# q and k of tiles 4 to 15 by seven products a pair, softmax and h lows partly on POOL, in an attention and MLP kernel

## The chip, the cores and the metric

The kernel runs on one core of one Trainium2 chip. The core has a matrix engine (PE; its weight loads are listed as PEld), a vector engine (DVE), an activation engine (ACT), a general engine (POOL, GpSimd) and SyncE (SP), which here only issues DMAs; ACT issues some as well. Each engine works through its own list of instructions in order. The metric is the device time of one execution in microseconds (us); the three runs of the kernel before have a median of 498.23 us (497.23 to 498.86).

## The reference, cut to what matters

```python
def _A_ref(x, wqkv, wo):                       # x: [1, 2048, 512]
    H = 32; Dh = D // H; W, dil = 8, 2         # 32 heads of 16
    q, k, v = split(x @ wqkv)
    ... # position s sees s, s-2, ... s-14
    logits = einsum("bhsd,bhswd->bhsw", q, kg) * Dh ** -0.5
    attn = softmax(where(mask, logits, -1e9))
    return einsum("bhsw,bhswd->bhsd", attn, vg) @ wo

def _B_ref(x, w1, b1, w2, b2):                 # 1792 hidden
    h = x @ w1 + b1
    return relu(h) ** 2 @ w2 + b2

xn = _layernorm(x)
return x + _A_ref(xn, wqkv, wo) * silu(_B_ref(xn, w1, b1, w2, b2))
```

## The kernel before

The 2048 rows are cut into 16 tiles of 128. To keep fp32 accuracy, every operand of a product is split into a high part (rounded by ACT to the matrix engine's fp32r) and a low part, the rest (a subtraction, mostly on DVE). A product is then three matmuls (`PASSES`): high by high, high by low, low by high.

**The pair stage.** For each tile the statistics and the normalised x are made, x is transposed (from tile 4 on: four DMAs that move blocks, `shuffle`, then a 32x32 block transpose on DVE, `trans`), split into high and low (`lowx`), and multiplied by the weights of q, k and v: 12 matmuls of 128x512 each (`qkv`). Tiles are worked on in pairs; two tiles together are a unit of 256 rows, whose q, k and v go to DRAM (`sq`, `sk`, `sv`).

**Attention** runs on DVE alone, unit by unit. For one unit there are four slices for the logits (`qk`: a 128x2048 multiply `pr`, then a reduce into `L`), the softmax (`soft_a`: row maximum `mx`, subtraction, exp on ACT; `soft_b`: row sum `sm`, reciprocal, product), and four slices for the weighted sum (`av`: a multiply `pv`, a reduce into `v`). The finished unit is stored to DRAM (`so`), loaded again in another layout (`oq`, four DMAs, `load_o`), transposed on DVE (`trans_o`, tiles `pT`), split (`lowo`, tiles `oT`) and multiplied by wo on PE (`out_product`, tiles `pw`).

**The MLP stage.** Four chunks of 512 rows, each over 14 blocks f of the hidden layer: `up` (12 matmuls into `ph`; then relu, square into the high part of `h` and the full square on ACT), `lowh` (the low part of h, on DVE), `down` (12 matmuls into the four banks `pb`, two blocks behind). At the end of a chunk the four gates are made (z = pb + b2 on DVE, silu on ACT); later z is multiplied by `pw` on DVE and x is added on POOL, and the result stored. Blocks 0 and 1 of the first chunk run in the last pair.

**What sets the order.** Each engine keeps the order in which the code calls it. The attention is a generator (`attention`); `pump` takes steps from it as long as a running count of DVE's work is not ahead of PE's. So the place of an attention step in DVE's list is fixed when the program is built, by that count.

The weights w1 and w2 of a block are loaded into four shared buffers (`piece`) and split once; the blocks below NKEEP = 6 during the pairs, the others in the first chunk.

Of the kernel before, what the change touches and what calls it, by code (L numbers as in the profile page):

```python
# [14 lines left out]
P = 128  # L15
# [20 lines left out]
NKEEP = 6  # L36
# [14 lines left out]
def body(ctx: ExitStack, tc: tile.TileContext, x, wqkv, wo, w1, b1, w2, b2, out):  # L51
# [38 lines left out]

    const = ctx.enter_context(tc.tile_pool(name="const", bufs=1))
# [3 lines left out]
    keep = ctx.enter_context(tc.tile_pool(name="keep", bufs=1))  # L95
    hpool = ctx.enter_context(tc.tile_pool(name="ph", bufs=1))
# [24 lines left out]
    ident = const.tile([P, P], F32, name="ident")  # L121
# [4 lines left out]

    p1ctx = ExitStack()
    px, pstg, pwq, pxT = (p1ctx.enter_context(tc.tile_pool(name=n, bufs=1)) for n in ("px", "pstg", "pwq", "pxT"))
    xins = {}
# [6 lines left out]
    def load_x(t):  # L136
        xins[t] = px.tile([P, D], F32, name=f"x{t}", tag="x", bufs=4)
        dma(xins[t], tile_rows(x, t))

    wq = [pwq.tile([P, 2, KT, 512], FR, name=f"wq{s}") for s in range(3)]  # L140
# [15 lines left out]
    def wq_parts(s, kt):  # L156
        return wq[s][:, 0, kt], wq[s][:, 1, kt], raws[s, kt]
# [66 lines left out]
    def attention():  # L224
# [30 lines left out]
        def soft_a(u, h=None):  # L255
            yield 1500
            m = part(u, h)
            L, n = Ls[u][:, m], m.stop - m.start
            if u == 0:
                i = slice(m.start // 8, m.stop // 8)  # L260
                lm = L.rearrange("p (i h) w -> p i h w", h=8)
                V.tensor_add(lm, lm, mask[:, i, None, :].to_broadcast([P, n // 8, 8, W]))
            mx = att.tile([P, n], F32, name=f"mx{u}_{h}", tag="mx")
            V.tensor_reduce(out=mx, in_=L, axis=AX.X, op=OP.max)
            V.tensor_sub(L, L, mx[:, :, None].to_broadcast([P, n, W]))

            def exp():
                A.activation(L, L, AF.Exp)
                exps.add((u, h))

            defer(clock["V"] + BEHIND, exp)

        def soft_b(u, h=None):
            while (u, h) not in exps:
                yield None
            yield 2100
# [90 lines left out]
    def load_w(pool, f):  # L367
        w12[f] = pool.tile([P, 2, 2, 512], FR, name=f"w{f}")

        r1, r2 = (p2.tile([P, 512], F32, name=f"{n}{f}", tag="xr", bufs=2) if f in (6, 9) else piece(f"{n}{f}")  # L370
                  for n in ("w1r", "w2r"))
# [4 lines left out]
    def split_w(f, eng=G):  # L376
        for i, r in enumerate(raws.pop(f)):
            split(w12[f][:, 0, i], w12[f][:, 1, i], r, eng)
# [3 lines left out]
    mv, means, rs, shifts, xn, xb, pTs, xt, xT, seen = ({} for _ in range(10))  # L382

    def moments(t, st):
        mv[t] = px.tile([P, 2], F32, name=f"mv{t}", tag="mv", bufs=2)
        rs[t] = px.tile([P, 1], F32, name=f"rs{t}", tag="rs", bufs=3)
        V.bn_aggr(mv[t], st)
        V.tensor_scalar_add(rs[t], mv[t][:, 1:2], 1e-5)
        G.tensor_tensor(rs[t], rs[t], mhalf, op=OP.pow)

    def small(name, t):
        return px.tile([P, 1], F32, name=f"{name}{t}", tag=name, bufs=3)

    def scratch(t):
        return px.tile([P, D], F32, name=f"scratch{t}", tag="scratch")

    def mean(t):
        means[t] = small("mean", t)
        A.activation(scratch(t), xins[t], AF.Copy, accum_out=means[t])
        G.tensor_scalar(means[t], means[t], -1.0 / D, None, op0=OP.mult)  # L400

    def spread(t):
        rs[t], shifts[t] = small("rs", t), small("shift", t)
        A.activation(scratch(t), xins[t], AF.Square, bias=means[t], accum_out=rs[t])
# [9 lines left out]
    def norm(t):  # L414

        src = xins.pop(t)
        if t < TURN:
            xn[t] = dst = px.tile([P, 2, D], F32, name=f"xn{t}", tag="xn", bufs=2)[:, 0]
# [11 lines left out]
        if t + 4 < NT:  # L430
            load_x(t + 4)
# [7 lines left out]
    def shuffle(t):  # L439

        src = xn.pop(t)
        xb[t] = px.tile([P, 4, 2, P], F32, name=f"xb{t}", tag="xn", bufs=2)
        for a in range(4):
            dma(xb[t][32 * a:32 * a + 32].rearrange("p b e c -> p b (e c)"), src[:, a].rearrange("p e c -> p (e c)"))

    def trans(t):
# [6 lines left out]
        else:  # L453
# [3 lines left out]
            seen[t] = clock["V"] + 800  # L457
        A.activation(xt[t][:, 0], pTs[t].rearrange("p (k n) -> p k n", k=KT), AF.Copy)

    def lowx(t):  # L460
        not_before(seen.pop(t))
        V.tensor_sub(xt[t][:, 1], pTs.pop(t).rearrange("p (k n) -> p k n", k=KT), xt[t][:, 0].bitcast(F32))

    stgs = {}

    def qkv(t, s, between=None, late=False):
# [5 lines left out]
        for n, (kt, a, b) in enumerate(order):  # L472
            PE.matmul(ps, xt[t][:, a, kt], wq[s][:, b, kt, :], start=n == 0, stop=n == 11)
# [4 lines left out]
    def evacuate(t, s, ps):  # L478
        if t % 2 == 0:
            stgs[s] = pstg.tile([P, 4, 2, P], F32, name=f"stg{t}_{s}", tag="stg", bufs=4)  # L480
        A.activation(stgs[s][:, :, t % 2], ps.rearrange("p (g c) -> p g c", g=4), AF.Copy,
                     scale=0.25 if s == 0 else 1.0)
        if t % 2:
            r0 = (t - 1) * P + (0 if s == 0 else HALO)
            dst = (sq, sk, sv)[s][:, r0:r0 + UP, :].rearrange("g (p e) c -> p g (e c)", e=2)
            dma(dst, stgs[s].rearrange("p g e c -> p g (e c)"))
            done = done_tiles["qkv"[s]]
            done[0] = t + 1
            done[1][t // 2] = clock["PE"]
# [8 lines left out]
    def up(c, f):  # L498
# [12 lines left out]
        A.activation(ph, ph, AF.Square)  # L511
        hs[f] = h, ph, clock["PE"] + 2000

    def lowh(f):
        h, ph, t = hs[f]
        not_before(t)
        V.tensor_sub(h[:, 1], ph, h[:, 0].bitcast(F32))
# [21 lines left out]
    x0 = scratch(0)  # L539
# [25 lines left out]
    for f in range(2):  # L565
        load_w(keep, f)
# [4 lines left out]
    lowx(2)  # L571
    qkv(1, 0, lambda: highs(2, 2))
    trans(3)
    lows(2, 2)
    lowx(3)
    stats(4)
    stats(5)
    next(stream)
    qkv(0, 2)
    norm(4)  # L580
    norm(5)
    shuffle(4)
    split_w(0, V)
    pump(LATE)
    qkv(1, 2)
    split_w(1, V)
    pump(LATE)
    for a in range(2, NT, 2):
        b, more = a + 1, a + 2 < NT
        later = a + 4 < NT  # L590

        def weights(f):
            if 2 <= f < NKEEP:
                load_w(keep, f)
            if 2 <= f - 1 < NKEEP:
                split_w(f - 1)

        if later:
            mean(a + 4)
        qkv(a, 0)  # L600
        if a + 2 < TURN:
            trans(a + 2)
        if later:
            spread(a + 4)
            mean(b + 4)
        pump(LATE)
        qkv(b, 0)
        weights(a - 5)
        if a + 2 < TURN:
            lowx(a + 2)  # L610
            trans(b + 2)
        elif more:
            trans(a + 2)
        if later:
            norm(a + 4)
            spread(b + 4)
        pump(LATE)
        qkv(a, 1)
        if a + 2 < TURN:
            lowx(b + 2)  # L620
        elif more:
            lowx(a + 2)
            trans(b + 2)
        if later:
            norm(b + 4)
            shuffle(a + 4)
        pump(LATE)
        if not more:
            up(0, 0)
        qkv(b, 1)  # L630
        if TURN <= a + 2 < NT:
            lowx(b + 2)
        if not more:
            pump()
            up(0, 1)
            lowh(0)
        weights(b - 5)
        pump(LATE)
        qkv(a, 2)
        pump(LATE)  # L640
        qkv(b, 2)
        if a == NT - 4:
            dma(b1t, b1.rearrange("(f p) -> p f", p=P))
        if a >= TPC:
            for t in (a, b):
                dma(sx[t // TPC][:, t % TPC], xt.pop(t).bitcast(F32))
        pump(LATE if more else -SLACK)
# [73 lines left out]
    dma(b2t, b2[None, :].to_broadcast([P, D]))  # L721

    for c in range(NCH):
# [4 lines left out]
        for f in range(2, NF):  # L728
            if c == 0:
                for i in (6, 7) if f == 2 else (f + 5,):  # L730
                    if i < NF:
                        load_w(p2, i)
            up(c, f)
            pump()
            if c == 0 and f == 3:
# [6 lines left out]
            if c == 0:  # L742
                if NKEEP <= f + 3 < NF:
                    split_w(f + 3)
# [100 lines left out]
```

## Time and profile before

| | |
|---|---|
| median of three runs | 498.23 us (497.23 to 498.86) |
| the profiled execution | 495.58 us |
| its span, first to last instruction | 493.8 us |
| mean granted PE clock | 0.998 |
| pair stage, to the end of the last pair | about 146 us |
| first gate of chunk 0, 1, 2 on DVE | 220.8, 305.8, 392.8 us |
| last attention reduce ends | 460.5 us |

The profile gives for every engine its busy time, in windows if asked; the chain that ended last, which follows each wait back to what released it; groups of equal instructions with their mean; and the single instructions in order of time, each with its start, its duration and the idle time before it. In these rows a name such as `pr<-k,q` says which tile is written from which others, without buffer numbers.

### The profile page before, as it was taken

How to read it: one execution, taken by the hardware profiler on the slowest of the kernel's cores; microseconds unless marked ns; L12 is line 12 of the kernel's file. 1: busy time of each engine (PE TensorE's matmuls, PEld its weight loads, DVE VectorE, ACT ScalarE, POOL GpSimd, SP SyncE). 2: the span in 40 equal slices, each digit the busy share in tenths (PEclk: the TensorE clock that was granted, in tenths of full speed). 3: DMA queues.
4: the chain of work that ended last, by engine and by line, in shares of the span. 5: the costliest groups of instructions: out<-in, count | busy, mean ns of one | idle time of the engine just before them, and what ended most of it. 6: DMA issues, size and time to landing. Idle time of an engine off the chain costs nothing.

```text
span 493.8 us, 5860 instructions
## 1 busy us (share of the span) xinstructions
PE 487.5 (99%) x2154; PEld 401.1 (81%) x2154; DVE 431.7 (87%) x370; ACT 211.0 (43%) x377; POOL 97.9 (20%) x105
## 2 busy tenths in 40 slices
PE   8999999999999999999999999999999999999997
PEld 5888888888888888887888888888888888888886
DVE  5925798998999999998999998899999889999445
ACT  5636455563343665316333324432252354313331
POOL 1311015571000779300112000112100011220000
PEclk9999999999999999999999999999999999999999
DMA  7999979769977892653406408043241805030222
GB/s 287 297 287 341 304 238 313 225 238 323 372 228 262 203 274 65 202 212 118 127 31 216 181 22 329 4 164 123 85 161 43 328 2 202 1 127 1 85 85 86
DMA packets 48520, 88.79 MB, mean 180 GB/s; under 512 B 5372, under 2 KB 32364, under 8 KB 45676
## 3 DMA queue, kind: packets, MB, share of 16 engines
q1 hardware_dynamic: 44172, 54.87, 35.3%
q10 hardware_dynamic: 4320, 33.56, 19.1%
q8 instruction: 17, 0.28, 0.2%
q14 instruction: 11, 0.09, 0.1%
HBM read 57.94 MB, written 27.32 MB: 173 GB/s over the span
## 4 chain that ended last, share of the span: by engine, by line
PE 83%; DVE 9%; issue 4%; ACT 2%; DMA 1%; ACTq 0%; POOL 0%; DVEq 0%; POOLq 0%
PE pq L80 27%; PE ph L80 24%; PE pb L80 24%; PE pw L80 8%; DVE v L80 2%; DVE pr L80 2%; DVE h L80 2%; DVE pv L80 1%; DMA x<-in_A_x 1%; ACT ph L80 0%; DVE sm_None L80 0%; ACT z L80 0%; DVE z L80 0%; ACT h L80 0%; PE pxT L80 0%
## 5 line engine op out<-in xcount | busy, mean ns | idle before, releaser
L80 PE MATMUL pb<-w,h 128*128 128x512 f32 x672 | 160.6, 389 | 0.0
L80 PEld LDWEIGHTS pb<-w,h 128*128 128x128 f32 x672 | 126.1, 188 | 26.2
L80 PE MATMUL ph<-xU,w 128*128 128x512 f32 x504 | 120.7, 389 | 0.3 <-DVE h L80 0.3
L80 PEld LDWEIGHTS ph<-xU,w 128*128 128x128 f32 x504 | 94.6, 188 | 20.2 <-DVE h L80 0.7
L80 ACT ACTIVATE ph<-ph,b1t 128x512 f32<-128x512 f32 x56 | 37.0, 661 | 163.0 <-PE ph L80 158.4
L80 PE MATMUL pq<-wq,xt 128*128 128x512 f32 x432 | 98.7, 390 | 0.0
L80 PEld LDWEIGHTS pq<-wq,xt 128*128 128x128 f32 x432 | 81.0, 188 | 17.2 <-ACT stg L80 0.3
L80 DVE TENSOR_TENSOR pr<-k,q 128x2048 f32<-128x2048 f32 x32 | 75.4, 2356 | 0.3
L80 DVE TENSOR_TENSOR pv<-v,L 128x2048 f32<-128x2048 f32 x32 | 73.8, 2305 | 0.4
L80 DVE TENSOR_REDUCE L<-pr 128x128 f32<-128x2048 f32 x32 | 72.9, 2279 | 0.6
L80 DVE TENSOR_REDUCE v<-pv 128x256 f32<-128x2048 f32 x32 | 72.9, 2279 | 0.6
L80 POOL TENSOR_TENSOR z<-z,xr 128x512 f32<-128x512 f32 x12 | 23.2, 1936 | 214.7 <-DVE z L80 209.9
L80 DVE TENSOR_TENSOR h<-ph,h 128x512 fp32r<-128x512 f32 x56 | 38.3, 683 | 19.9 <-ACT ph L80 19.9
L80 PE MATMUL pw<-wot,oT 128*128 128x512 f32 (+1 forms) x204 | 45.9, 376 | 0.0
L80 PEld LDWEIGHTS pw<-wot,oT 128*128 128x128 f32 x204 | 36.8, 188 | 7.1
L80 PE MATMUL ph<-xT,w 128*128 128x512 f32 x168 | 40.7, 391 | 0.0
L80 ACT ACTIVATE stg<-pq 128x512 f32<-128x512 f32 x48 | 27.2, 595 | 26.4 <-PE pq L80 16.9
L80 PEld LDWEIGHTS ph<-xT,w 128*128 128x128 f32 x168 | 31.5, 188 | 7.0 <-DVE h L80 0.4
L80 ACT ACTIVATE h<-ph 128x512 fp32r<-128x512 f32 x56 | 33.7, 601 | 1.8
L80 ACT ACTIVATE ph<-ph 128x512 f32<-128x512 f32 x56 | 33.3, 595 | 0.0
L80 PE MATMUL pq<-wq,xT 128*128 128x512 f32 x132 | 31.7, 398 | 0.0
L80 POOL TENSOR_TENSOR w<-w1r,w 128x512 fp32r<-128x512 f32 x12 | 18.9, 1577 | 57.1 <-DMA rwo<-in_A_wo 48.8
(66 smaller groups left out, 309.9 us busy)
## 6 DMA issues: line engine op xcount, KB each, us to landing
k<-sk ACTq DMA_DIRECT2D x8, 1408.0 KB, 8.1
v<-sv ACTq DMA_DIRECT2D x8, 1408.0 KB, 8.3
sx<-xt SPq DMA_DIRECT2D x12, 512.0 KB, 5.5
xU<-sx ACTq DMA_DIRECT2D x6, 1024.0 KB, 5.4
x<-in_A_x SPq DMA_DIRECT2D x16, 256.0 KB, 5.0
sk<-stg SPq DMA_DIRECT2D x8, 512.0 KB, 7.1
sq<-stg SPq DMA_DIRECT2D x8, 512.0 KB, 5.6
q<-sq ACTq DMA_DIRECT2D x8, 512.0 KB, 8.4
```

Of the source, the lines that this page charges most:

```text
L80: return tc.keep_in_program_order(f(*a, **k))
```

## The change

Four parts.

1. For the pairs of tiles 4 to 15, q and k come from seven half-size products (`SEVEN`, `pair_of_seven`) in place of eight. The two tiles are the rows, the halves of the 512 inputs the inner blocks, q and k the columns of a 2x2 block product. Needed are four sums of x blocks (`sums`: 128x256 each on DVE, split again by `high_sums` and `low_sums`), four sums of weight blocks (made once, on DVE), and seven additions of 128x512 for each pair (five on DVE out of PSUM, two on POOL). v is computed as before.
2. The work for later tiles is put into six steps of a pair by a table (`plan`), and the sums of the next pair are made one pair ahead.
3. The statistics from tile 6 on take the mean's factor on ACT, and no POOL operation for it (`spread`).
4. Blocks of x are loaded sooner and in order on SP (`queue`, `load_x` in `shuffle`); statistics and norms of tiles 4 and 5 are made earlier; the buffers of the q, k and v weights are used again for w1 and w2 (`HOME`), which are loaded and split two blocks ahead (`next_w`).

In the MLP stage the low part of h is made on POOL for chunks 1 to 3, from a copy of the square in SBUF (`hf`), and for whole units the softmax's subtraction and product go to POOL. The factor 0.25 of the logits moves from q into the exp.

```diff
         def soft_a(u, h=None):
-            V.tensor_sub(L, L, mx[:, :, None].to_broadcast([P, n, W]))
+            (G if h is None else V).tensor_sub(L, L, mx[:, :, None].to_broadcast([P, n, W]))
...
         def soft_b(u, h=None):
-            V.tensor_mul(L, L, sm[:, :, None].to_broadcast([P, n, W]))
+            (G if h is None else V).tensor_mul(L, L, sm[:, :, None].to_broadcast([P, n, W]))
...
+    def next_w():
+        f = len(w12)
+        if f < NF:
+            w12[f] = buffer(f"w{f}", HOME[f]) if f in HOME else p2.tile([P, 2, 2, 512], FR, name=f"w{f}")
+            for i, r in enumerate(raws.pop(f)):
+                split(w12[f][:, 0, i], w12[f][:, 1, i], r, G)
+            if f + 2 < NF:
+                load_w(f + 2)
...
+    def sums(a, half):
+        f, (pa, pb) = Sf[a], quarters(a)
+        if half == 0:
+            not_before(seen[a, "copy"])
+            V.tensor_add(f[:, 0], f[:, 3], pb[:, 1])
+            V.tensor_sub(f[:, 1], f[:, 0], pa[:, 0])
+        else:
+            V.tensor_sub(f[:, 2], pa[:, 0], f[:, 3])
+            V.tensor_sub(f[:, 3], pa[:, 1], f[:, 1])
...
+    def product(a, n, lhs, w):
+        ps = psA(f"pm{a}_{n}")
+        k = 0
+        for i in range(2):
+            for p, q in PASSES:
+                PE.matmul(ps, lhs(p, i), wq[w][:, q, i, :], start=k == 0, stop=k == 5)
+                k += 1
...
     def up(c, f):
-        A.activation(ph, ph, AF.Square)
-        hs[f] = h, ph, clock["PE"] + 2000
...
+        full = hpool.tile([P, 512], F32, name=f"hf{c}_{f}", tag="hf") if c else ph
+        A.activation(full, ph, AF.Square)
+        if c:
+            G.tensor_sub(h[:, 1], full, h[:, 0].bitcast(F32))
+        hs[f] = h, None if c else ph, clock["PE"] + 2000
...
     norm(3)
     lowx(2)
+    stats(4)
     qkv(1, 0, lambda: highs(2, 2))
     trans(3)
+    stats(5)
+    norm(4)
     lows(2, 2)
+    norm(5)
+    shuffle(4)
     lowx(3)
...
+    def pair_of_seven(a):
...
+        q, k = stgs[0], stgs[1]
+        p = product(a, 1, part_x(a, 0), Q0)
+        A.activation(q[:, :, 0], p, AF.Copy)
+        p = product(a, 5, part_s(a, 0), T1)
+        A.activation(k[:, :, 1], p, AF.Copy)
+        beside(a, 0)
+        p = product(a, 6, part_s(a, 1), T2)
+        not_before(clock["PE"])
+        V.tensor_add(k[:, :, 0], q[:, :, 0], p)
+        p = product(a, 2, part_x(a, 1), Q1)
+        beside(a, 1)
+        not_before(clock["PE"])
+        V.tensor_add(q[:, :, 0], q[:, :, 0], p)
+        p = product(a, 7, part_s(a, 2), T3)
+        not_before(clock["PE"])
+        V.tensor_add(q[:, :, 1], k[:, :, 0], p)
+        G.tensor_add(k[:, :, 0], k[:, :, 0], k[:, :, 1])
+        G.tensor_add(k[:, :, 1], k[:, :, 1], q[:, :, 1])
+        p = product(a, 3, part_s(a, 3), K1)
+        beside(a, 2)
+        qkv(a, 2)
+        not_before(clock["PE"] - 12 * MATMUL)
+        V.tensor_add(k[:, :, 0], k[:, :, 0], p)
+        store_qkv(b, 1)
+        beside(a, 3)
+        p = product(a, 4, part_x(b, 1), T4)
+        beside(a, 4)
+        not_before(clock["PE"])
+        V.tensor_add(q[:, :, 1], q[:, :, 1], p)
+        store_qkv(b, 0)
+        if last:
+            for f in range(2):
+                up(0, f)
+                pump()
+            lowh(0)
+        qkv(b, 2)
+        beside(a, 5)
```

(`beside(a, step)` makes what the table has for that step and pumps.) Three places of the programs show how instructions move. First PE's list at the pair of tiles 4 and 5: `pq4_0` is q of tile 4, `pm4_5` the fifth product of the pair that begins with tile 4, `S4_0` the first two sums of x. Before:

```order
L80 MATMUL pq4_0_537<-wq0_111,xt4_440 128x512 x12
L80 MATMUL pq5_0_564<-wq0_111,xt5_471 128x512 x12
L80 MATMUL pq4_1_596<-wq1_112,xt4_440 128x512 x12
L80 MATMUL pq5_1_625<-wq1_112,xt5_471 128x512 x12
L80 MATMUL pq4_2_645<-wq2_113,xt4_440 128x512 x12
L80 MATMUL pq5_2_662<-wq2_113,xt5_471 128x512 x12
```

And of the change:

```order
L84 MATMUL pm4_1_586<-wq0_111,xt4_473 128x512 x6
L84 MATMUL pm4_5_594<-wq6_117,S4_0_530 128x512 x6
L84 MATMUL pm4_6_606<-wq7_118,S4_0_530 128x512 x6
L84 MATMUL pm4_2_614<-wq1_112,xt4_473 128x512 x6
L84 MATMUL pm4_7_643<-wq8_119,S4_1_561 128x512 x6
L84 MATMUL pm4_3_653<-wq3_114,S4_1_561 128x512 x6
L84 MATMUL pq4_2_676<-wq4_115,xt4_473 128x512 x6
L84 MATMUL pq4_2_676<-wq5_116,xt4_473 128x512 x6
L84 MATMUL pm4_4_699<-wq9_120,xt5_476 128x512 x6
L84 MATMUL pq5_2_727<-wq4_115,xt5_476 128x512 x6
L84 MATMUL pq5_2_727<-wq5_116,xt5_476 128x512 x6
```

Four times 12 matmuls for q and k became seven times 6, and the second product of the pair already needs the sums.

Second, DVE's list at the first gate, the end of chunk 0: `z0_0` is the gate of its first tile, `v2` and `pv2` belong to attention unit 2. Before:

```order
L80 TENSOR_TENSOR pv2_3_1982<-v2_1650,L2_1245 128x4x2x256
L80 TENSOR_REDUCE v2_1650<-pv2_3_1982 128x256
L80 TENSOR_REDUCE sm3_None_2012<-L3_1626 128x64
L80 RECIPROCAL sm3_None_2012<-sm3_None_2012 128x64
L80 TENSOR_TENSOR L3_1626<-L3_1626,sm3_None_2012 128x512
L80 TENSOR_TENSOR z0_0_2017<-pb0_0_1440,b2t_1438 128x512
```

And of the change:

```order
L84 TENSOR_REDUCE v1_1747<-pv1_1_2035 128x256
L84 TENSOR_TENSOR pv1_2_2062<-v1_1747,L1_1374 128x4x2x256
L84 TENSOR_TENSOR z0_0_2064<-pb0_0_1484,b2t_1483 128x512
L84 TENSOR_TENSOR z0_1_2067<-pb0_1_1485,b2t_1483 128x512
L84 TENSOR_TENSOR z0_2_2070<-pb0_2_1486,b2t_1483 128x512
L84 TENSOR_TENSOR z0_3_2073<-pb0_3_1487,b2t_1483 128x512
L84 TENSOR_REDUCE v1_1747<-pv1_2_2062 128x256
L84 TENSOR_TENSOR pv1_3_2115<-v1_1747,L1_1374 128x4x2x256
L84 TENSOR_REDUCE v1_1747<-pv1_3_2115 128x256
```

The attention stands one unit further back at this place: unit 1 is being finished where unit 2 was done.

Third, DVE's list where the output of unit 6 is transposed for tiles 12 and 13 (`pT12<-oq6`), in chunk 3. Before, the last reduce of unit 6 (`v6`) stands 15 rows ahead of the transposes, and these rows lead up to them:

```order
L80 TENSOR_TENSOR pv7_1_3588<-v7_3376,L7_3140 128x4x2x256
L80 TENSOR_REDUCE v7_3376<-pv7_1_3588 128x256
L80 TENSOR_TENSOR h3_8_3572<-ph3_8_3559,h3_8_3572 128x512
L80 TENSOR_TENSOR pv7_2_3621<-v7_3376,L7_3140 128x4x2x256
L80 TENSOR_REDUCE v7_3376<-pv7_2_3621 128x256
L80 TENSOR_TENSOR h3_9_3605<-ph3_9_3592,h3_9_3605 128x512
L80 STREAM_TRANSPOSE pT12_3642<-oq6_3538 128x4x4x32
L80 STREAM_TRANSPOSE pT13_3646<-oq6_3538 128x4x4x32
```

And of the change:

```order
L84 TENSOR_TENSOR pv6_3_3733<-v6_3496,L6_3108 128x4x2x256
L84 TENSOR_REDUCE v6_3496<-pv6_3_3733 128x256
L84 TENSOR_REDUCE sm7_None_3737<-L7_3432 128x64
L84 RECIPROCAL sm7_None_3737<-sm7_None_3737 128x64
L84 STREAM_TRANSPOSE pT12_3777<-oq6_3741 128x4x4x32
L84 STREAM_TRANSPOSE pT13_3781<-oq6_3741 128x4x4x32
```

The transposes now stand two rows behind the last reduce of the unit that they transpose, and the h lows between the slices are gone from DVE's list. The same place for units 2 to 5 has three or four rows between.

More of the change, by code (lines that the diff above doesn't have):

```diff
@@ L137, in load_x, with buffer @@
         xins[t] = px.tile([P, D], F32, name=f"x{t}", tag="x", bufs=4)
-        dma(xins[t], tile_rows(x, t))
-    wq = [pwq.tile([P, 2, KT, 512], FR, name=f"wq{s}") for s in range(3)]
+        queue(xins[t], tile_rows(x, t))
+    def buffer(name, i):
+        return wts.tile([P, 2, 2, 512], FR, name=name, tag=f"b{i}")
+    wq = [buffer(f"wq{i}", i) for i in range(10)]
     raws = {}
@@ L365, in body, with load_w @@
     w12 = {}
[L367 to L371, printed above, removed]
+    def load_w(f):
+        r1, r2 = (piece(f"{n}{f}") for n in ("w1r", "w2r"))
         dma(r1.rearrange("p (k c) -> p k c", c=P), w1[:, f * P:(f + 1) * P].rearrange("(k p) c -> p k c", p=P))
@@ L441, in shuffle, with trans @@
         src = xn.pop(t)
[L442 removed]
+        xb[t] = px.tile([P, 4, 2, P], F32, name=f"xb{t}", tag="xb", bufs=2)
         for a in range(4):
[L444 to L446 removed]
+            queue(xb[t][32 * a:32 * a + 32].rearrange("p b e c -> p b (e c)"), src[:, a].rearrange("p e c -> p (e c)"))
+        for i in range(6 if t == TURN else t + 4, min(t + 6, NT)):
+            load_x(i)
+    def trans(t, then=True):
         place(t)
@@ L564, in body @@
     constants()
-    for f in range(2):
-        load_w(keep, f)
     qkv(0, 0, lambda: highs(2, 0))
@@ L584, in body, with at @@
+    sum_weights = [(wq[w][:, 0, i], wq[w][:, 1, i], raws[s, kt + i])
+                   for w, (s, kt) in ((T1, (0, 0)), (T2, (1, 2)), (T3, (1, 0)), (T4, (0, 2))) for i in range(2)]
+    for w in sum_weights[:4]:
+        split(*w, V)
     pump(LATE)
     qkv(1, 2)
-    split_w(1, V)
+    for w in sum_weights[4:]:
+        split(*w, V)
     pump(LATE)
+    plan = {}
+    def at(a, step, f, *args):
+        if args[0] < NT:
+            plan.setdefault((a, step), []).append((f, args))
     for a in range(2, NT, 2):
[L589 to L605, printed above, removed]
-        pump(LATE)
[L607 to L635, printed above, removed]
-            lowh(0)
-        weights(b - 5)
-        pump(LATE)
-        qkv(a, 2)
-        pump(LATE)
-        qkv(b, 2)
@@ new lines, in body, with beside @@
+    for t in range(6, NT, 2):
+        for i, (a, step) in enumerate({6: ((2, 0), (2, 1), (2, 2), (2, 3)), 8: ((2, 4), (2, 5), (4, 0), (4, 1))}.get(
+                t, ((t - 6, 1), (t - 6, 2), (t - 6, 4), (t - 6, 5)))):
+            at(a, step, (spread, spread, norm, norm)[i], t + i % 2)
+            if i == 3:
+                at(a, step, shuffle, t)
+    ahead = {4: 1, 6: 1, 14: 2}
+    def beside(a, step):
+        for f, args in plan.get((a, step), ()):
+            f(*args)
+        if step == 4:
+            for n in range(ahead.get(a, 0)):
+                next_w()
+        pump(LATE)
@@ L642, in body @@
+    for a in range(2, NT, 2):
+        if a >= TPC:
+            for t in (a, a + 1):
+                dma(sx[t // TPC][:, t % TPC], xt[t].bitcast(F32))
+        (pair_of_seven if a in SEVEN else pair)(a)
+        if a == 2:
+            load_w(0)
+            load_w(1)
         if a == NT - 4:
             dma(b1t, b1.rearrange("(f p) -> p f", p=P))
[L644 to L647, printed above, removed]
+    pump()
```

158 lines of the change are left out of this document (105 added, 53 removed).

## The prediction

> **What bounds the kernel now.** I read the page's shares first, then the chain that ended last, then DVE's own order of time.
>
> ```profile
> span 493.8 us, 5860 instructions
> ...
> PE 487.5 (99%) x2154; PEld 401.1 (81%) x2154; DVE 431.7 (87%) x370; ACT 211.0 (43%) x377; POOL 97.9 (20%) x105
> ...
> PE 83%; DVE 9%; issue 4%; ACT 2%; DMA 1%; ACTq 0%; POOL 0%; DVEq 0%; POOLq 0%
> ```
>
> PE is busy for 99% of the span and carries 83% of the chain: a matmul fewer is time gained, as long as nothing else becomes late. DVE is the candidate for that, and the windows show how close it is.
>
> ```profile
> 30.00:60.00 30.00, 30.00 (x132) 24.51 (x131) 14.51 (x14) 15.37 (x32) 4.36 (x15) 1.00 1.01 312
> 60.00:90.00 30.00, 30.00 (x134) 24.86 (x133) 26.94 (x27) 15.41 (x36) 9.78 (x17) 1.00 0.91 286
> ...
> 150.00:200.00 50.00, 50.00 (x221) 41.11 (x220) 49.66 (x34) 28.51 (x52) 33.29 (x19) 1.00 0.68 195
> ```
>
> After the length the columns are PE, PEld, DVE, ACT, POOL. DVE has half of its time free up to 60 us and next to none later; ACT and POOL have room. Next the pace of DVE, start to start (and above it the last 24 down products of chunk 0 on PE).
>
> ```profile
> 214.52 5.60 PE L80 MATMUL pb<-w,h 128*128 128x512 f32 x24
> ...
> 218.86 0.68 DVE L80 TENSOR_REDUCE sm_None<-L 128x64 f32<-128x512 f32 x1
> 219.57 0.55 DVE L80 RECIPROCAL sm_None<-sm_None 128x64 f32<-128x64 f32 x1
> ...
> 220.16 0.69 DVE L80 TENSOR_TENSOR L<-L,sm_None 128x512 f32<-128x512 f32 x1
> 220.77 2.48 DVE L80 TENSOR_TENSOR z<-pb,b2t 128x512 f32<-128x512 f32 x4
> ...
> 441.05 0.68 DVE L80 TENSOR_TENSOR h<-ph,h 128x512 fp32r<-128x512 f32 x1
> 441.64 2.28 DVE L80 TENSOR_TENSOR pv<-v,L 128x2048 f32<-128x2048 f32 x1
> 443.96 2.29 DVE L80 TENSOR_REDUCE v<-pv 128x256 f32<-128x2048 f32 x1
> 446.16 0.68 DVE L80 TENSOR_TENSOR h<-ph,h 128x512 fp32r<-128x512 f32 x1
> ```
>
> A 128x512 operation takes DVE 0.60, an attention multiply 2.32, its reduce 2.20 (a slice 4.52), a row maximum or sum 0.71, a reciprocal 0.59. The first gate (z = pb + b2) stands at 220.77. From there to the last attention reduce, which ends at 460.54 (row below), DVE's order holds 36 slices, 83 operations of 0.60, 12 transposes of 0.65, 8 maxima and sums and 4 reciprocals: 162.7 + 49.8 + 7.8 + 5.7 + 2.4 = 228.4 us of 239.8. So DVE has 11.4 us to spare there and spends it waiting, mostly here:
>
> ```profile
> DVE h L80 <- ACT ph L80: 19.9, 10, 4.8
> ```
>
> **PE's gain.** Six pairs go from 72 matmuls to 42 + 24 = 66.
>
> ```profile
> 20.12 112.45 PE pq L80 x492
> ```
>
> 492 matmuls in 112.45 us are 0.2286 us each; 36 fewer give 8.2 us.
>
> **PE's losses in the pair stage.** The change puts the statistics of tiles 4 and 5 and the first norm on DVE ahead of the low halves of v's second weight buffer.
>
> ```profile
> 19.20 1.28 DVE L80 TENSOR_TENSOR wq<-wqraw,wq 128x512 fp32r<-128x512 f32 x2
> ...
> 19.87 22.73 PE L80 MATMUL pq<-wq,xT 128*128 128x512 f32 x96
> ...
> 21.44 0.68 DVE L80 BATCH_NORM_STATS2 st<-x 128x6 f32<-128x512 f32 x1
> ...
> 22.45 0.69 DVE L80 BATCH_NORM_STATS2 st<-x 128x6 f32<-128x512 f32 x1
> ...
> 23.46 0.54 DVE L80 TENSOR_SCALAR xn<-x,mv,rs 128x512 f32<-128x512 f32 x1
> ```
>
> One tile's statistics take 1.01 (21.44 to 22.45), a norm 0.54: 2.6 us go ahead of lows that began at 19.20, so the first is done at 22.4. PE needs it for the eighth matmul after 19.87, at 21.5. Loss 0.9 to 1.2, I take 1.2 (0 to 2.6).
> In each pair DVE must now do 9 operations of 0.60 (two lows of x, two of the sums, five combinations), 4 of 0.42 (the 128x256 sums) and two transposes: 8.4 of the pair's 66 x 0.2286 = 15.1 us. That leaves room for one slice and some softmax, and the order has one slice in a pair where it had about two. Summed along the order at these paces, the sums are ready just ahead of the second product except in tiles 6 and 7, half a microsecond late: 0.5 (0 to 6, one late operation in each pair). I take 1.7 us for the stage. ACT's quarter copies, highs and spreads, POOL's two additions a pair, the weights split two steps ahead instead of three and the earlier x cost nothing: ACT is busy 15.4 of 30 us, POOL 9.8. Were that cover gone, the addition that waits for POOL would cost a POOL operation, 1.3 us (below), in each of six pairs.
> Up to here the span would be 493.8 - 8.2 + 1.7 = 487.3.
>
> **DVE after the first gate.** Of the 24 products from 214.52 on, the fifteenth ends the first gate's bank, 15 x 0.227 and the drain later, at 218.1; DVE took it up at 220.77. PE is now 6.5 us sooner: 211.6. DVE comes there in step: in chunk 0 its order has two h lows with no slice between, where it waits for PE. But the pairs have put off slices: 45 multiplies and 46 reduces are still to do there. The 39 h lows and 8 subtractions and products of the softmax have gone to POOL. Left are 45 x 2.32 + 46 x 2.20 = 205.6, 36 operations of 0.60 (21.6), 12 transposes (7.8), 11 maxima and sums (7.8), 6 reciprocals (3.5): 246.3 us, 17.9 more than before.
>
> **Stalls at the output transposes.** This is the largest new term.
>
> ```profile
> 458.26 2.28 DVE L80 TENSOR_REDUCE v<-pv 128x256 f32<-128x2048 f32 x1
> ...
> 460.56 0.53 SPq L304 DMA_DIRECT2D so<-v  x1
> ...
> 463.67 1.74 SPq L676 DMA_DIRECT2D oq<-so  x4
> ...
> 473.38 1.31 DVE L80 STREAM_TRANSPOSE pT<-oq 128x512 f32<-128x512 f32 x2
> ...
> 484.36 5.75 PE L80 MATMUL pw<-wot,oT 128*128 128x512 f32 x36
> ```
>
> ```profile
> DMA to landing us min/median/max: 2.3/3.1/10.0
> ```
>
> (The single row is that of oq's loads.) A unit's output goes through DRAM: the store is issued at the end of the last reduce, the first load 3.1 us later, the fourth 1.3 after the first, and it lands 3.1 later (2.3 at least): 7.5 us, at least 6.7. Before, DVE had the whole of another unit's work between. In the new order the transposes stand almost behind the reduce: for unit 6 only a sum and a reciprocal lie between (1.3 us), for unit 5 those and one 0.60 (1.9), unit 4 a multiply (3.6), unit 3 one 0.60 more (4.2), unit 2 a slice (5.8). DVE works in order, so the rest is idle: at 7.3 us 6.0 + 5.4 + 3.7 + 3.1 + 1.5 = 19.7. For unit 1 a store of z, waiting for POOL, stands between on SP: 3 (0 to 5). Sum 22.7; 16.7 with 6.7 and nothing for unit 1, 26 with 7.5 and 5.
>
> The Trainium skill (DMA: Bandwidth & Descriptors, "Anatomy of one DMA") gives a DMA a fixed cost of about 2.0 us. By an estimate from that figure, store and load would be 2.0 + 1.3 + 2.0 = 5.3, the stalls 10.2 where I have 19.7, the last load 2.0 sooner, and the span about 498 instead of 509.6; the trace has 3.1 us for either transfer and never under 2.3 for a load, so I keep the trace.
>
> **Collisions of DVE and POOL.** POOL now gets 42 h lows, and the softmax operations.
>
> ```profile
> 188.52 1.30 POOL L80 TENSOR_TENSOR w<-w2r,w 128x512 fp32r<-128x512 f32 x1
> ...
> 189.00 2.97 DVE L80 TENSOR_TENSOR pr<-k,q 128x2048 f32<-128x2048 f32 x1
> ...
> 189.77 3.35 POOL L80 TENSOR_TENSOR wot<-rwo,wot 128x512 fp32r<-128x512 f32 x1
> ```
>
> ```profile
> L80 DVE TENSOR_TENSOR pr<-k,q 128x2048 f32<-128x2048 f32 x32 | 75.4, 2356 | 0.3
> ```
>
> POOL needs 1.30 alone, but 3.35 when it comes during a multiply, and the multiply takes 2.97 for 2.28 when it comes during POOL's: they don't run together. The 32 multiplies' mean of 2356 ns over 2280 is 2.4 us; with the L operations about 4 us for POOL's 40 large ones, 0.1 each. After the gate POOL has 42 + 11 + 12 = 65: 6.5 us, between 0 and 65 x 0.69 = 45. I take 6.5, the observed rate.
>
> **The sum.** The last reduce ends at 211.6 + 246.3 + 22.7 + 6.5 = 487.1. Behind it:
>
> ```profile
> 478.51 0.69 DVE L80 TENSOR_TENSOR z<-pb,b2t 128x512 f32<-128x512 f32 x1 [0.79 <-PE pb L80]
> ...
> 483.94 1.38 DVE L80 TENSOR_TENSOR z<-pb,b2t 128x512 f32<-128x512 f32 x2
> ...
> 490.60 0.42 DVE L80 TENSOR_TENSOR z<-z,xlast 128x256 f32<-128x256 f32 x1
> ```
>
> 7.3 to land, 2.6 for transposes, copies and lows, 6.8 for the last gates (478.51 to 485.3), 3.0 for the last products (two of 0.6, four of 0.42), 2.8 from 491.0 to the span's end: 22.5. The span is **509.6**, 15.8 over before. The profiled execution took 495.58 around its 493.8, and the median of the runs is 498.23, 4.4 over the span; so 514.
>
> **Rivals.**
> - *PE stays the bound*, the other side: all that DVE waits and collides for fits into its room. For 487.3 the last reduce must end by 464.8, 6.9 us more than 211.6 + 246.3. For: h lows no longer stand in DVE's order, and POOL is idle. Against: the transposes alone stall 16.7 at the least. It decides in the five transposes' idle time: under 7 with the collisions, and the time is 487.3 + 4.4 = **491.7**.
> - *Break-even*: stalls and collisions together 13.4 us (last reduce at 471.3): 498. It needs loads faster than any in the trace and no collision.
> - *POOL becomes late*: its softmax operations wait for DVE in the same queue as the h lows, of which a down product needs each about 9 us after ACT. If DVE is over 9 us late when it hands over a row sum, PE waits for POOL as well, and collisions run towards 0.69 each; half of them would be 22 us: 509.6 + 16 + 4.4 = **530**.
>
> **How the numbers follow.** Forecast 0.74, PE bound 0.16, break-even 0.04, POOL late 0.06. The forecast's own range: no collisions and stalls of 16.7 give 211.6 + 246.3 + 16.7 + 22.5 = 497.1, in this measure 501.5; stalls of 26 and 14 of collisions give 520.4, or 525. It holds most of 0.74; to leave out no more than 2 in 10 the range reaches to break-even at 498 and, past the late POOL, to 531, and leaves out the bound PE. Within 0.3% (1.5 us, about what can be told from no change) is the break-even case.
>
> **What would show it.** Right: DVE idle in front of the transposes, ended by the load of oq, 1 to 6 us each and about 20 in all; the first gate near 212; the last reduce near 487, and DVE's share of the chain several times its 9%. Wrong: these idle times absent or the first gate under 205 (then the rival's 491.7); PE waiting in the pairs for S or stg by more than 6 us (the pair stage missized); multiplies with a mean over 2600 ns (collisions missized).

## The result and the profile after

The changed kernel takes 543.99 us (median of four runs, 542.01 to 546.34) against 498.55: 1.0922 times as long, with a 95% interval of 1.0884 to 1.0959. The prediction had 514.0 and a range of 498 to 531; the direction was right, the size was not. The profiled execution took 542.01, its span is 540.2.

The page of the changed kernel, its span, its busy times and the shares of the chain that ended last:

```profile
span 540.2 us, 5913 instructions
...
PE 496.2 (92%) x2118; PEld 404.5 (75%) x2118; DVE 449.5 (83%) x392; ACT 218.9 (41%) x391; POOL 202.6 (37%) x167
...
DVE 45%; PE 28%; DMA 14%; issue 5%; SPq 3%; POOL 2%; ACT 2%; ACTq 0%; DVEq 0%; POOLq 0%
```

PE has 36 matmuls fewer and is no longer the bound: the chain has gone to DVE (9% before) and to DMA (1% before). Yet DVE is busy for a smaller share of the span than before, so it waits on that chain. Its view of waits (for whom, us in total, times, longest) says where:

```profile
DVE pT L84 <- DMA oq<-so: 52.7, 7, 8.7
```

Before, no transpose of an output waited. Now seven pairs of transposes do, each for the load that brings the unit's output back from DRAM. DVE's own order shows the first gate, unit 2's last steps with its transposes, and the end of the attention:

```profile
214.72 2.29 DVE L84 TENSOR_TENSOR pv<-v,L 128x2048 f32<-128x2048 f32 x1
216.93 2.48 DVE L84 TENSOR_TENSOR z<-pb,b2t 128x512 f32<-128x512 f32 x4
...
275.38 2.29 DVE L84 TENSOR_REDUCE v<-pv 128x256 f32<-128x2048 f32 x1
277.58 0.68 DVE L84 TENSOR_REDUCE sm_None<-L 128x64 f32<-128x512 f32 x1
278.29 0.55 DVE L84 RECIPROCAL sm_None<-sm_None 128x64 f32<-128x64 f32 x1
278.76 2.23 DVE L84 TENSOR_TENSOR pr<-k,q 128x2048 f32<-128x2048 f32 x1
281.02 2.29 DVE L84 TENSOR_REDUCE L<-pr 128x128 f32<-128x2048 f32 x1
289.79 1.32 DVE L84 STREAM_TRANSPOSE pT<-oq 128x512 f32<-128x512 f32 x2 [6.48 <-DMA oq<-so]
...
515.13 2.29 DVE L84 TENSOR_REDUCE v<-pv 128x256 f32<-128x2048 f32 x1
525.00 1.32 DVE L84 STREAM_TRANSPOSE pT<-oq 128x512 f32<-128x512 f32 x2 [7.59 <-DMA oq<-so]
```

The output of unit 2 is complete at 277.67; a sum, a reciprocal and one slice (5.6 us) stand ahead of its transposes, and then DVE idles 6.48. The round trip took 12.1 us, where the prediction had 7.3. SP's order and the chain show the legs of that trip for unit 2, and SP's order what happened to unit 1:

```profile
226.27 0.53 SPq L318 DMA_DIRECT2D so<-v  x1
233.17 0.35 SPq L855 DMA_DIRECT2D out<-z  x1
234.00 3.13 SPq L814 DMA_DIRECT2D oq<-so  x4
...
277.69 0.53 SPq L318 DMA_DIRECT2D so<-v  x1
280.74 1.76 SPq L814 DMA_DIRECT2D oq<-so  x4
```

```profile
277.69 2.98 DMA so<-v
...
282.07 7.59 DMA oq<-so
```

Unit 2's store took 3.0 us (3.1 predicted); its last load took 7.6 in place of 3.1. At unit 1 the loads stand on SP behind a store of z, which waits for POOL's addition: the first is issued 7.7 us after the store of the unit.

PE in turn now stops, and comes back slower. Its order at one such stop:

```profile
288.44 2.88 PE L84 MATMUL pb<-w,h 128*128 128x512 f32 x12
293.47 4.60 PE L84 MATMUL ph<-xU,w 128*128 128x512 f32 x12 [2.15 <-ACT hf L84]
```

### The profile page after: what moved, and what is told of

It is laid out like the page before. It is cut to its first block, busy times and chain, and to the rows that moved or that the text cites. A ratio compares the mean times of both kernels' runs of the same rounds, so it can differ in the third digit from the quotient of the medians.

```text
span 540.2 us, 5913 instructions
## 1 busy us (share of the span) xinstructions
PE 496.2 (92%) x2118; PEld 404.5 (75%) x2118; DVE 449.5 (83%) x392; ACT 218.9 (41%) x391; POOL 202.6 (37%) x167
## 4 chain that ended last, share of the span: by engine, by line
DVE 45%; PE 28%; DMA 14%; issue 5%; SPq 3%; POOL 2%; ACT 2%; ACTq 0%; DVEq 0%; POOLq 0%
DVE pv L84 11%; DVE v L84 10%; PE pm L84 9%; DVE pr L84 8%; DVE L L84 8%; PE ph L84 7%; DMA oq<-so 6%; PE pb L84 6%; PE pq L84 6%; DMA so<-v 4%; DVE z L84 3%; SPq L814 2%; DMA x<-in_A_x 2%; DVE oT L84 2%; DVE pT L84 2%
## 5 line engine op out<-in xcount | busy, mean ns | idle before, releaser
L84 PE MATMUL ph<-xU,w 128*128 128x512 f32 x504 | 127.4, 405 | 16.4 <-ACT hf L84 16.4
L84 POOL TENSOR_TENSOR h<-hf,h 128x512 fp32r<-128x512 f32 x42 | 72.1, 1716 | 141.9 <-ACT hf L84 121.3
L84 DVE TENSOR_TENSOR pv<-v,L 128x2048 f32<-128x2048 f32 x32 | 79.3, 2479 | 0.7
L84 PE MATMUL pw<-wot,oT 128*128 128x512 f32 (+1 forms) x204 | 53.0, 417 | 17.7 <-DVE oT L84 17.7
L84 DVE STREAM_TRANSPOSE pT<-oq 128x512 f32<-128x512 f32 x16 | 10.5, 705 | 52.7 <-DMA oq<-so 52.7
L84 ACT ACTIVATE oT<-pT 128x512 fp32r<-128x512 f32 x16 | 9.4, 597 | 76.5 <-DVE pT L84 76.5
L84 PE MATMUL pm<-wq,S 128*128 128x512 f32 x144 | 35.3, 395 | 0.0
L84 PE MATMUL pq<-wq,xt 128*128 128x512 f32 x144 | 34.6, 389 | 0.0
L84 PEld LDWEIGHTS pm<-wq,S 128*128 128x128 f32 x144 | 27.7, 192 | 5.9
L84 PEld LDWEIGHTS pq<-wq,xt 128*128 128x128 f32 x144 | 27.0, 188 | 5.6
```

The source lines that it names most:

```text
L84: return tc.keep_in_program_order(f(*a, **k))
```

## The experiments

Theory 1 is the prediction's: behind the first gate DVE is the bound, above all because a unit's transposes stand right behind its last reduce. The rivals: POOL's new operations (collisions with DVE, late h lows), and losses of the pairs of seven on PE. Where only a span is given, the kernel ran once.

**Slices ahead of the transposes.** The order is filled with other DVE work; nothing is removed.

```diff
+                pump(clock["V"] - clock["PE"] + 9300)
                 trans_o(t0 - 2, psT(f"pT{t0 - 2}"))
...
             if f == 10:
+                pump(clock["V"] - clock["PE"] + 9300)
```

> Two attention slices are taken ahead of every pair of output transposes; nothing else is changed. Theory 1 (DVE is the bound after the first gate, and what it loses there is its wait for oq at the transposes): the order now has 10 to 18 us of DVE work between a unit's last reduce and its transposes, and the round trips through DRAM took 8 to 14 us, so the six waits of 6.5 to 8.7 us (45.1 us) go, only the one behind the last unit (7.6) stays; span 540.2 - 45 = 495 us, between 491 and 502. Theory 2 (the operations that went to POOL cost the time, by collisions with DVE and as late h lows for PE): the same POOL operations run, the waits come back under other names; span over 525. Theory 3 (the two parts of DVE's wait hide PE's own wait for oT): the span falls by less than half, 515 to 525.

Measured: 505.26 us, 1.0121 times before (1.0082 to 1.016); span 503.4. DVE's wait for oq fell from 52.7 to 9.0, of which 7.5 behind the last unit:

```profile
DVE pT L84 <- DMA oq<-so: 9.0, 2, 7.5
```

That is 37 of the 46 us lost, from an edit that only changes the order. The span is 8 us more than the 495 expected. One cause is that the fill in chunk 0 stood ahead of h lows: PE waited 4.6 us for one, and the first gate came at 223.57, 6.6 later than in the changed kernel. The next run leaves this fill out.

> As the run with two slices ahead of the transposes, but not for unit 0, in chunk 0, where the slices stood ahead of h lows that PE waits for. Theory 1: first gate back at 217, 246 us of work, 9 of collisions, no wait for oq but the last (7.6, in the 22.8 behind the last reduce): span 495, between 492 and 499. Rival (what was left of the loss in that run are waits between PE and DVE in every chunk): span 500 to 505 as there.

```diff
             if f == 10:
+                if c:
+                    pump(clock["V"] - clock["PE"] + 9300)
```

Measured: 501.44 us, 1.0061 (1.0042 to 1.008); span 499.5, half a microsecond past what was expected. DVE's first gate and last reduce:

```profile
217.45 2.48 DVE L84 TENSOR_TENSOR z<-pb,b2t 128x512 f32<-128x512 f32 x4
...
474.57 2.29 DVE L84 TENSOR_REDUCE v<-pv 128x256 f32<-128x2048 f32 x1
```

The last reduce ends at 476.86, 22.6 before the end. Between the two lie 259.4 us, with 1.6 of waiting for oq and 1.2 for POOL's softmax product. So 246.3 of work ran in 256.6: 10.3 us, not 9, were lost, 8.1 of them in the 45 multiplies, which took 2.46 on average where 2.28 is usual.

**Fewer pairs of seven.** First none (`SEVEN = ()`, no sums of weights, two homes of w1 and w2 exchanged), then the four pairs from tile 8 on.

> q and k of every tile are made as before the change (no pair of seven, no sums of weights); POOL's h lows and softmax, the table of steps, the earlier blocks of x stay. Theory 1 (seven products put 10 slices behind the first gate, so that units end just ahead of their transposes): DVE has 35 multiplies left at the first gate in place of 45 and over 25 us of work between every unit's last reduce and its transposes but the last's; no wait for oq, PE bound again with all 2154 matmuls, span 491 to 498. Theory 2 (POOL's new operations cost it): they are all still there, span over 520.

Measured: 497.2 us, 0.9956 (0.9932 to 0.9979); span 493.2, no wait for oq, PE 96% of the chain. POOL's h lows and its softmax operations are all still there (of its new work only the twelve additions of the pairs are gone), so they are not by themselves what made the change slow.

```diff
-SEVEN = range(4, 16, 2)
+SEVEN = range(8, 16, 2)
-    ahead = {4: 1, 6: 1, 14: 2}
+    ahead = {4: 1, 8: 1, 14: 2}
```

> Seven products only for the pairs from tile 8 on (four pairs, 24 matmuls less than before). Theory 1: 41 multiplies at the first gate, 20 us and more of DVE work between a unit's last reduce and its transposes, so no wait for oq but a short one behind unit 7; PE bound: 493.8 - 24 x 0.227 = 488.3 and up to 4 of losses in the pairs: span 488 to 493, faster than the kernel before by 0.3 to 1%. Theory 2 (POOL's operations): span over 515. Theory 3 (the pairs of seven lose on PE by themselves what they save): span 493 to 498.

Measured: 491.23 us, **0.9856 times before (0.982 to 0.9892)**; the fastest kernel of this study. Its page and DVE's last reduce:

```profile
span 489.5 us, 5904 instructions
...
PE 93%; DMA 3%; DVE 2%; ACT 0%; issue 0%; POOL 0%; ACTq 0%; SPq 0%; POOLq 0%
```

```profile
450.26 2.29 DVE L84 TENSOR_REDUCE v<-pv 128x256 f32<-128x2048 f32 x1
```

The attention is done 37 us before the end, against 23 in the changed kernel, and the span is 4.3 us below that of the kernel before, where 24 matmuls are worth 5.5. Not all of the 1.4% belongs to the pairs: the kernel without any was already 0.4% faster than before, so the four pairs account for about 1.2% (491.23 against 497.2). Then five pairs, with the fill for units 1 to 7 and the later statistics of the run described below.

> Seven products from tile 6 on (five pairs, 30 matmuls less than before), with two slices ahead of the transposes of units 1 to 7 and the later statistics of tiles 10 and 11. Theory 1: 43 multiplies at the first gate, 19 us and more between a unit's last reduce and its transposes (2.5 for the last unit): PE bound at 493.8 - 30 x 0.227 = 487.0 and 0 to 3 of losses: span 487 to 490, 0.8 to 1.4% faster than before, about as the four pairs or 1 us better. Rival (DVE is the bound again, 214 + 236 + 9 + 22.8 = 482 and every wait on top): span over 491.

Measured: 497.2 us, 0.9967 (0.9938 to 0.9996); span 495.6, a miss. In chunk 3 DVE waits for POOL's softmax product, unit 7 ends at 464.5, and PE stops:

```profile
445.62 2.29 DVE L84 TENSOR_TENSOR pv<-v,L 128x2048 f32<-128x2048 f32 x1 [3.91 <-POOL L L84]
...
471.99 0.73 DVE L84 STREAM_TRANSPOSE pT<-oq 128x512 f32<-128x512 f32 x1 [4.86 <-DMA oq<-so]
```

```profile
468.12 4.59 PE L84 MATMUL ph<-xU,w 128*128 128x512 f32 x12 [2.29 <-ACT hf L84]
```

The last gates begin at 480.22, 6.0 later than with four pairs: the difference of the two spans. By these rows DVE and PE are too close with five pairs, and the last unit, with nothing left to fill in, decides; no run separates the fifth pair from the fill and the later statistics that came with it.

**h lows back on DVE.**

```diff
-        full = hpool.tile([P, 512], F32, name=f"hf{c}_{f}", tag="hf") if c else ph
+        full = ph
-        if c:
-            G.tensor_sub(h[:, 1], full, h[:, 0].bitcast(F32))
```

> The low part of h of chunks 1 to 3 goes back from POOL to DVE. Theory 1 (DVE bound, collisions small): 39 x 0.60 = 23.4 us more on DVE, some 5 us of collisions less, waits for oq as they are or longer: span 553 to 565. Theory 2 (the POOL lows collide with the multiplies and are late for PE, and that is the loss): span under 535.

Measured: span 582.5, 42.3 more than the change, where 13 to 25 were expected. PE's waits and one of PE's stops:

```profile
PE ph L84 <- DVE h L84: 64.5, 12, 21.5
```

```profile
458.41 5.37 PE L84 MATMUL ph<-xU,w 128*128 128x512 f32 x12 [17.36 <-DVE h L84]
```

The h lows stand behind several slices of attention on DVE, PE waits for them, and DVE then for ph (these waits rose from 9.3 to 38.8). So the lows on POOL cost some DVE time, and save more.

**What lengthens the round trip.** The load of the next unit's v (1408 KB) becomes free with the same last reduce as the store; here it is issued about two blocks later.

```diff
+VFREE = 12000
...
-                defer(max(clock["V"] + FREE if u else 0, done_tiles[n][1][u] + LAND), start)
+                defer(max(clock["V"] + (VFREE if n == "v" else FREE) if u else 0, done_tiles[n][1][u] + LAND), start)
```

> The changed kernel with the load of the next unit's v (1408 KB, on ACT's queue) issued about two blocks later, behind the copies of the transposed output on ACT. Theory 1 (it is this load, set free by the same last reduce as the store, that slows oq's loads): oq lands 2.8 to 3.2 us after its fourth issue for units 1 to 4 in place of 4.2, 7.6, 8.2 and 6.0; the order has 2.3 us less of other work ahead of the transposes of units 3 and 4, so the waits for oq fall from 52.7 to about 43 us and the span from 540 to about 530 (526 to 534). Rival (the loads are slow of themselves, or by another transfer): oq lands as late as before, waits 52 to 58 us, span 538 to 546.

Measured: span 531.9, as expected, waits 45.7. The DMA issues around unit 2's trip, of the changed kernel and of this one (KB each, median us to landing):

```profile
v<-sv ACTq DMA_DIRECT2D x1, 1408.0 KB
...
oq<-so SPq DMA_DIRECT2D x4, 128.0 KB, 7.4
```

```profile
oq<-so SPq DMA_DIRECT2D x4, 128.0 KB, 2.8
```

Units 1, 3 and 5 kept trips of 10 us and more; a store of z stood between on SP. The next edit calls `load_o` ahead of `finish`:

> The changed kernel with the load of an odd unit's output (oq) issued ahead of the first finished z of the chunk before, on SP; in the changed kernel oq of unit 1 was issued 7.7 us after the store (234.0 against 226.27), behind a store of z that waited for POOL. Theory (the queue is what makes unit 1's round trip 14 us): oq of unit 1 is issued 3 to 4.5 us behind its store, DVE's wait ahead of those transposes falls from 7.0 to 3 to 4.5, the other waits stay within 1 us: all waits 48.5 to 51, span 536 to 539. Rival (the store itself, or the transfers that run beside, set it): the wait stays over 6, span 539 to 543.

Measured: span 547.6, waits 56.9. SP's order is set by a scheduler, and it left z's store between for unit 1 (oq again 7.74 behind its store), so this did not test the expectation; for unit 5, where the store of so now came ahead of z's, the wait rose from 7.5 to 12.2: its loads, issued from 444.69 on, came 1.5 us behind v's load and took 7.6 to 7.8.

> The changed kernel with the finished z of all but the last tiles stored by POOL's own queue, so that nothing that waits for POOL stands between the store of a unit's output and the load of oq on SP (the run before this one left that order on SP as it was for unit 1). Theory: oq of unit 1 is issued 3 to 4.5 us behind its store in place of 7.7, DVE's wait there falls from 7.0 to 2 to 4, unit 5's by 1; all waits for oq 46 to 50 in place of 52.7, span 533 to 538. Rival (transfers that run beside set unit 1's round trip): its wait stays over 6, span 539 and over.

```diff
-        dma(tile_rows(out, t)[:, cols], z[:, cols])
+        (G.dma_start if eng is G else dma)(tile_rows(out, t)[:, cols], z[:, cols])
```

Measured: span 541.9, unit 1's wait 6.5: a miss. In z's place stood the next load on SP that waits for the same addition of POOL, that of xr, whose buffer it frees:

```profile
225.40 0.53 SPq L318 DMA_DIRECT2D so<-v  x1
232.30 0.33 SPq L847 DMA_DIRECT2D xr<-in_A_x  x1
233.13 2.76 SPq L814 DMA_DIRECT2D oq<-so  x4
```

> The same with v's load two blocks later as well; the transposes stay where the change puts them. Theory (queue and v's load are what made the round trips longer than the prediction's 7.3 us): every round trip from last reduce to the landing of oq is 7.3 to 9 us; the order has 7.1, 5.9, 1.9, 1.3, 1.9 and 1.3 us of work inside them for units 1 to 6, so the waits are about 1, 2, 6, 7, 6 and 7, and 7.5 for unit 7: 36 in all (33 to 40), span 521 to 528. Rival (something else lengthens them): waits over 43, span over 530.

Measured: span 534.9, waits 46.2, a miss; the odd units again stood behind xr. At last xr's loads went to POOL's queue too (`G.dma_start` in `load_r`):

> v's load two blocks later, and both the stores of z and the loads of xr on POOL's own queue, so that on SP the loads of oq follow the store of so directly for every unit. Theory (v's load and the DMAs on SP that wait for POOL are all that lengthens the round trips): 7.2 to 8 us from last reduce to the transposes for every unit, waits of about 1, 1.6, 5.7, 6.2, 5.8, 6.2 and 7.3 us, 33.7 in all (31 to 37); the transposes stay where the change puts them, span 540.2 - 19 = 521, between 517 and 526. Rival (something else lengthens them): round trips of units 1, 3 and 5 stay over 9 us, waits over 42, span over 529.

Measured: span 525.4, waits 36.7, both inside what was expected:

```profile
DVE pT L85 <- DMA oq<-so: 36.7, 7, 8.3
```

Times from the end of a unit's last reduce to its transposes, and the wait in it, from DVE's rows:

| unit | changed kernel: trip, wait | this run: trip, wait |
|---|---|---|
| 1 | 14.4, 7.0 | 8.9, 1.5 |
| 2 | 12.1, 6.5 | 7.6, 2.0 |
| 3 | 12.7, 8.7 | 7.4, 5.7 |
| 4 | 11.4, 8.0 | 9.5, 8.3 |
| 5 | 9.2, 7.5 | 7.4, 5.7 |
| 6 | 8.6, 7.4 | 7.3, 6.1 |
| 7 | 7.6, 7.6 | 7.3, 7.3 |

With v's load later and nothing on SP that waits for POOL, the trips of units 2, 3, 5 and 6 take 7.3 to 7.6 us, as the prediction had it. Units 1 and 4 keep 8.9 and 9.5, with 4.5 and 4.1 us from the store to the first load in place of 3.1; what slows them stays open. The trips of units 1 to 6 sum to 68.3 us in the changed kernel and to 48.2 here, where six of 7.3 are 43.8. So these two things together made most of the difference. The waits fell by less than the trips, since units 3 and 4 have 1.7 and 1.2 us of work inside theirs here, in place of 4.0 and 3.4.

**Statistics of tiles 10 and 11 three steps later.** In the changed kernel PE stops once in the pair of tiles 6 and 7. ACT's, DVE's and PE's rows there:

```profile
53.45 0.60 ACT L84 ACTIVATE mean<-x 128x512 f32<-128x512 f32 x1 [2.56 <-DMA x<-in_A_x]
...
57.47 0.69 DVE L84 TENSOR_TENSOR stg<-stg,pm 128x512 f32<-128x512 f32 x1 [3.12 <-POOL stg L84]
58.08 2.88 DVE L84 TENSOR_TENSOR pr<-k,q 128x2048 f32<-128x2048 f32 x1
60.88 0.68 DVE L84 TENSOR_TENSOR xt<-pxT,xt 128x512 fp32r<-128x512 f32 x1
...
61.61 2.07 PE L84 MATMUL pm<-wq,xt 128*128 128x512 f32 x4 [2.60 <-DVE xt L84]
63.48 3.58 PE L84 MATMUL pm<-wq,S 128*128 128x512 f32 x12
```

POOL's additions of the pair before are queued behind the statistics of tile 10, whose x lands late. DVE waits for them, then does a multiply, and only then the low half of x that PE needs.

```diff
...
+                                         10: ((4, 3), (4, 4), (4, 5), (4, 5))}.get(
...
```

> The changed kernel with the statistics and norms of tiles 10 and 11 three steps later in the pair, so that POOL makes the two additions of the pair of tiles 4 and 5 before it waits for those tiles' x. Theory (the additions queued behind the statistics made DVE wait 3.1 us and PE 2.6 with some slow products behind it): both waits are gone, first gate at 213 to 214.5, span 535 to 538. Rival (the wait moves to the next thing that is late in that pair): first gate 216 to 217.5, span 539 to 542.

Measured: 542.81 us, span 540.2. DVE's wait for POOL and PE's stop are gone and the first gate is at 214.89, 2.0 earlier; but the waits for oq grew from 52.7 to 54.7, and the span is the same. The cause is found, its gain is lost again further on.

**All mends on six pairs.**

> All six pairs of seven, with the two slices ahead of the transposes of units 1 to 7, the later statistics of tiles 10 and 11, and oq ahead of z on SP: every wait found so far taken away but that behind the last unit. Theory (what is left is DVE's own work): first gate 214.9, 246.3 us of work and 11 of collisions with POOL, 22.8 behind the last reduce: span 495, between 493 and 498, so no faster than before by more than 0.2%, and above the four pairs' 489.5. Rival (the waits were the whole loss, and PE is the bound again): span 487 to 491.

Measured: 499.92 us, 1.0016 (0.9992 to 1.0039); span 496.8 (for the odd units the edit again left SP's order as it was, which behind the fill costs 2.6 us of waiting at most). With its waits gone the change is level with the kernel before. From the first gate at 213.84 to the end of the last reduce at 474.05 DVE idles only 4.5 us, while PE carries 76% of the chain again: with six pairs neither engine has room, and DVE's work and the 22.7 behind the last reduce fill the time that 36 matmuls would have saved.

## Why the prediction missed its range

Against the predicted span of 509.6 the measured 540.2 has 30.6 us more. By the prediction's own terms:

| term | predicted | measured |
|---|---|---|
| first gate on DVE | 211.6 | 216.93 |
| DVE's work from there | 246.3 | 246.3 and 9.1 of collisions = 255.4 |
| collisions | 6.5 | (in the row above) |
| stalls at the transposes, units 1 to 6 | 22.7 | 45.1 |
| behind the last reduce | 22.5 | 22.8 |

- **The bound.** That DVE takes it over from PE at the first gate was right, and the rival of a bound PE was wrong: PE is 28% of the chain.
- **The stalls** are the step that failed, by its size: 22.4 of the 30.6 us. Which work stands between last reduce and transposes was right to two tenths of a microsecond (trip less wait in the table), and the store's 3.1 was near (3.0 for units 2 to 4, 3.9 and 4.3 for units 5 and 6). Wrong was "the fourth [load] ... lands 3.1 later", taken as the same for all units. That was the median of the kernel before, where DVE waited for none of these loads. Now store and v load start from one event, and the later loads of oq of units 2 to 4 take 6.0 to 8.7 us beside it; on SP a DMA that waits for POOL goes ahead. The upper bound of 26 had 7.5 us for a trip where up to 12.7 were measured, and 5 of stall for unit 1, which had 7.0. The loads' maximum of 10.0, in the row that was quoted, was the sign that was passed over.
- **The pair stage** lost about 4.7 instead of 1.7. Its first stop on PE, and the last 24 products of chunk 0, which begin 3.5 us sooner than before, not 6.5:

```profile
22.70 20.53 PE L84 MATMUL pq<-wq,xT 128*128 128x512 f32 x89 [0.81 <-DVE wq L84]
...
211.06 5.60 PE L84 MATMUL pb<-w,h 128*128 128x512 f32 x24
```

- Of that loss the wait for v's weights, 0.81, was near the 0.9 to 1.2. "POOL's two additions a pair ... cost nothing" failed: POOL was seen as free by its busy time, but it works in order, and waited for statistics. "Were that cover gone" had 1.3 us; it was 2.6 for PE, and 1.7 for slower products: the 16 of the two rows shown took 5.4 us to the end, where 3.8 are usual.
- **The gate itself** came another 2.3 us late: when the bank's fifteenth product ended (211.06 + 15 x 0.227 = 214.5), DVE's order still had a multiply ahead of it, begun at 214.72. DVE did not come there in step, as assumed.
- **Collisions** were 9.1 for 6.5, as what is left of the 255.4 us. Of the 45 multiplies behind the gate 27 ran beside a POOL operation of over 0.9 us and took 2.57 us on average, the other 18 took 2.29: 7.6 of the 9.1. The multiplies' groups (mean ns) over the whole span, 2356 for pr and 2305 for pv before, are now:

```profile
L84 DVE TENSOR_TENSOR pv<-v,L 128x2048 f32<-128x2048 f32 x32 | 79.3, 2479 | 0.7
L84 DVE TENSOR_TENSOR pr<-k,q 128x2048 f32<-128x2048 f32 x32 | 78.9, 2467 | 0.4
```

- **The rival of a late POOL** was seen in other forms than forecast: as SP's loads behind z, and as DVE's 3.91 in the run with five pairs. **Break-even** was reached with six pairs only by the run with all mends.
- The sentence on the Trainium skill (DMA: Bandwidth & Descriptors, "Anatomy of one DMA") used its fixed 2.0 us alone. That section gives the cost for DMAs that GpSimd issues, and these are SP's. With its second term, the bytes over 436 GB/s, an estimate for the 512 KB store and a 128 KB load is 3.2 and 2.3 us, with 1.8 for the four issues 7.3 in all: the undisturbed trips of the table (7.3 and 7.4) agree.

## What to carry to other kernels

When work is moved off the bound, list what the next engine waits for in its new order, and price each wait with everything that the same event sets free: the store, the large load into the buffer just read, and what stands in the same queue. A queue is not free because its engine is idle; look at what its next instruction waits for. And a good part of a change may be worth more than the whole: with four pairs of seven products the kernel gains 1.4% (0.4% of it without any), with six it loses 9%, because the second engine's slack is used up in between.

## What was not expected of the hardware

A stop of PE can cost more than its length. Behind the waits of 2.15 and 2.29 us in the rows above the next 12 products took 4.60 and 4.59 us in place of 2.88, and behind a longer wait of the changed kernel no more:

```profile
426.50 4.61 PE L84 MATMUL ph<-xU,w 128*128 128x512 f32 x12 [3.85 <-ACT hf L84]
```

That is 1.7 us for each of these stops. The granted clock goes with it: behind the first it was 0.50 from 293.62 on for 3.41 us, and then 1.00 again. But the length of a wait does not settle its price. Of the changed kernel's nine waits of over 2 us eight were followed by slow products, 12 of them taking 4.4 to 5.5 us; behind one of 2.50, at 500.27, they took 3.04, at a granted clock of 1.00. The windows' rows from 340 to 360 us, where a wait of 4.33 cost 2.6, of the changed kernel and of the one before (length, then the five engines as in the prediction, granted clock, DMA share, GB/s):

```profile
340.00:360.00 20.00, 15.68 (x59) 12.41 (x58) 17.58 (x11) 6.33 (x11) 4.68 (x3) 0.83 0.12 32
```

```profile
340.00:360.00 20.00, 20.00 (x90) 16.58 (x89) 19.83 (x16) 5.26 (x9) 4.52 (x2) 1.00 0.24 70
```

So PE is busy 496.2 us for 36 matmuls fewer, where before it was busy 487.5. The Trainium skill (TensorE: Matmul & The Clock Gate, "Part 1: The HAM clock gate") has the clock halved after an idle window of about 3.4 us; here 2.15 us were enough once, and 2.50 were not another time.
